# The set-up of mask and selector, and the order of four early steps, in a fused block-sparse attention and SoLU layer

## The chip, the cores and the metric

One NeuronCore of a Trainium2 chip runs the whole program. Its engines work side by side, each in the order of its own queue: TensorE (PE, with weight loads shown as PEld), VectorE (DVE), ScalarE (ACT), GpSimd (POOL), and SyncE (SP), which here only issues transfers. They wait for each other by semaphores. The metric is the device time of one execution in microseconds, lower is better.

## The reference, cut to what matters

Attention over 4 batches, 8 heads, 768 tokens and a head width of 64. The mask works on blocks of 32 tokens (24 x 24 blocks): neighbours, the first and last row and column of blocks, and three sampled blocks in each row of blocks are kept. The result goes, as 3072 tokens x 512, through a layer that is softmax-gated and normalised.

```
mask = np.abs(blk_i - blk_j) <= 1
mask |= (blk_i == 0) | (blk_j == 0) | (blk_i == n_blocks-1) | (blk_j == n_blocks-1)
for qb in range(n_blocks):
    for kb in sampled_blocks[qb]: mask[block qb, block kb] = True
scores = where(mask, q @ k.T / 8, -1e9);  attn = softmax(scores);  x = attn @ v
h = x @ w_in;  solu = h * softmax(h)
out = ((solu - mean) / sqrt(var + 1e-6) * g_ln) @ w_out
```

## The kernel before, in words

**Tiling.** A batch has four pairs of heads (`pr`) and three passes of 256 queries; a pass has 12 units, three for each pair. A unit `s` is 256 keys x 256 queries of both heads: four matmuls into the tile `sco` (L400), one exp of 128 x 1024 on ACT (L411) into `exs`, and eight matmuls against the values into `op` (L428). There are 144 units. `normalise` (L441, L442) divides by the row sums and writes `xb`. Behind each pass follows the layer for its two groups of 128 tokens: `x_turn` transposes `xb` by DMA into `xT`, `h` by eight matmuls (L470), `e` = exp(h) on ACT (L479), `solu` = h times e on DVE (L491), its transpose by DMA into `lnT` (L496), statistics (L505) and the root `rstd` (DVE L512 to L521, then POOL L523), `o` by eight matmuls (L530), scaling by `rstd` on DVE (L541), a store.

**The mask as rows of the operands.** K transposed and Q transposed (`KT`, `QT`) have 64 rows for the head and 24 more. In KT these hold a selector (1 where the token lies in the row's block), in QT the mask of that query against each block of keys (0 or -30000), so the score matmul adds the mask by itself. `stat_m` is the static part of the mask (24 x 24); six selections on POOL (L593) make it. `selT` (24 x 768) is the selector, made from ones by two selections (L596). Three DVE operations on 24 x 24 (`acc`, L613 and L616) mark the sampled blocks once `samp_i` has come from memory; L618 multiplies them into `mask_l`. Two matmuls (L632) spread `mask_l` over 768 queries into `m_ps`; two ACT copies (L662) write that into the mask rows of QT for the two heads of pair 0. DVE copies (`mask_rows`, L644) write the rows of the other pairs from there, and `selT` into KT.

**Pair 0** is loaded first: ACT casts K's first two chunks of 128 tokens, K's other four, then Q's first two (L320); `turn_mm` transposes by matmuls (L350), `turn_out` copies the result out of PSUM on DVE (L322). Pairs 1 to 3 are cast on POOL; `selector(pr)` (L650) writes the selector into the natural layout of K there, so that the turn brings it along. `zeros` issues matmuls on zeros (L605) whose result nobody reads.

**The order.** Up to the first scores the order in the text is the order on each engine. From there a planner sorts steps by a due time in units of `s` (`at(when, ...)`); the sorted order is each engine's queue, and nothing is reordered later. Queues are in order: a step that waits holds back all that stands behind it on its engine. `p_h` and `p_o` are PSUM tiles with one buffer each: a turn, an `h` or an `o` that takes one waits until the tile before has been read. `sco` has two buffers. The transfers of SP, loads and transposes alike, stand in one queue too. For batch 1 the lists `first` give due times for loads, casts, DMA turns (`pd_k`, `pd_q`) and `shift` copies on POOL (L322) of each pair.

**The first group's statistics** (`stats`, `rstd` of group 0 of pass 0, the `head` case) are due at es + 4.1, es being the due time of its exp, 20.5. The second group's `solu` is due at 27.0.

Of the kernel before, what the change touches and what calls it, by code (L numbers as in the profile page):

```python
# [7 lines left out]
FP32 = mybir.dt.float32  # L8
# [200 lines left out]
def kernel(  # L209
# [14 lines left out]
    BLK = 32  # L224
# [332 lines left out]
    with tc.manual_schedule():  # L557
# [18 lines left out]
        nc.vector.memset(selT, 1.0)  # L576
# [8 lines left out]
        nc.gpsimd.tensor_copy(out=io_f, in_=io_i)  # L585
        nc.gpsimd.affine_select(out=ident, in_=ident, compare_op=ALU.not_equal, fill=1.0,
                                base=0, channel_multiplier=1, pattern=[[-1, 128]])
        for fill, base, cm, step in (
            (NEG, 1, -1, 1), (NEG, 1, 1, -1),
            (0.0, -1, 1, 0), (0.0, NB - 2, -1, 0),  # L590
            (0.0, -1, 0, 1), (0.0, NB - 2, 0, -1),
        ):
            nc.gpsimd.affine_select(out=stat_m, in_=stat_m, compare_op=ALU.is_ge, fill=fill,  # L593
                                    base=base, channel_multiplier=cm, pattern=[[step, NB]])
        for base, sg in ((0, 1), (BLK - 1, -1)):
            nc.gpsimd.affine_select(out=selT, in_=selT, compare_op=ALU.is_ge, fill=0.0,  # L596
                                    base=base, channel_multiplier=-BLK * sg,
                                    pattern=[[sg, NCH], [NCH * sg, TQ]])

        def zeros(n, pool=p_o):  # L600
            w = pool
            if pool in (p_o, p_op):
                w = pool.tile([128, 512], FP32, tag="o" if pool is p_o else "op", name="warm")
            for _ in range(n):
                nc.tensor.matmul(w, zer[:, 0:128], zer, start=True, stop=True,  # L605
                                 skip_group_check=True)

        zeros(8)
# [6 lines left out]
        for r in range(1, NR):  # L615
            nc.vector.scalar_tensor_tensor(out=acc[r], in0=io_f, scalar=samp_f[:, r : r + 1],  # L616
                                           in1=acc[r - 1], op0=ALU.is_equal, op1=ALU.max)
        nc.vector.scalar_tensor_tensor(out=mask_l[:, D:KR], in0=acc[-1], scalar=0.0, in1=stat_m,  # L618
# [6 lines left out]
        cast(nc.scalar, 0, 0, "k", 0, 2, 0)  # L625
        cast(nc.scalar, 0, 0, "k", 2, NCH, 0)
        cast(nc.scalar, 0, 0, "q", 0, 2, 0)
# [3 lines left out]
        for i in range(2):  # L631
            nc.tensor.matmul(m_ps[0:KR, i, 0 : S // 2], mask_l,  # L632
                             sel_f[:, i * (S // 2) : (i + 1) * (S // 2)], start=True, stop=True)

        def rows(t, h0, h1):
            return t[D:KR].rearrange("p (h c) t -> p h (c t)", c=NCH)[:, h0:h1]

        def spread(x, n):
            return x.rearrange("p (o c) -> p o c", o=1).broadcast_to([NB, n, S])
# [16 lines left out]
        warm_t = p_sco.tile([128, 2, 512], FP32, tag="sco", name="warm_t")[:, 0, :]  # L656
        zeros(1, warm_t)
        turn_mm(0, 0, "k", p_op, 2, NCH)
        zeros(1, warm_t)
        turn_out(0, 0, "k", DVE2, 0, 2)  # L660
        for hh in range(2):
            nc.scalar.copy(  # L662
                out=rows(QT[0], hh, hh + 1).rearrange("p o (i c) -> p (o i) c", i=2),
                in_=m_ps[D:KR, :, 0 : S // 2])
        turn_mm(0, 0, "q", p_o, 0, 2)
        zeros(3, warm_t)
# [13 lines left out]
        def turn(when, b, pr, key, pool, c0=0, c1=NCH, engs=DVE2, later=0.02):  # L680
            at(when, turn_mm, b, pr, key, pool, c0, c1)
            at(when + later, turn_out, b, pr, key, engs, c0, c1)
# [10 lines left out]
        for pr, w0 in ((2, 2.85), (3, 5.85)):  # L693
            selector(pr)
            cast(nc.gpsimd, 0, pr, "k")
            cast(nc.gpsimd, 0, pr, "q", 0, 2)
            turn(w0, 0, pr, "k", p_h)
            turn(w0 + 0.05, 0, pr, "q", p_o, 0, 2)
# [3 lines left out]
        for pr, when in enumerate((8.9, 10.9, 12.4, 15.4)):  # L702
            turn(when, 0, pr, "q", p_o, 2, NCH, later=0.06)
        at(4.5, nc.gpsimd.memset, mean_w, 1.0 / d_ff)
        at(4.5, nc.gpsimd.memset, ones_c, 1.0)
        at(4.5, nc.gpsimd.memset, mhalf, -0.5)
# [44 lines left out]
        for s in range(n_units):  # L751
# [15 lines left out]
            [9.1, 9.2, 9.3, 9.4, 9.5, 9.6, 24.1, 24.11], [9.5, 9.6, 14.0, 14.1, 14.2, 14.3, 26.8, 27.6],  # L767
            [12.5, 12.6, 24.05, 24.06, 27.1, 27.2, 33.2, 36.1],
            [17.0, 17.1, 26.0, 27.2, 29.2, 30.1, 36.6, 39.0],
            [9.7, 24.12, 27.3, 27.4], [18.0, 28.5, 32.0, 33.0])  # L770
# [16 lines left out]
        def layer(ps, i, hs, es, os):  # L787
            for when, n0, n1 in hs:
                at(when, h_mms, ps, i, n0, n1)
            at(es, e_exp, ps, i)  # L790
            head = ps == 0 and i == 0
            at(es + (0.33 if head else 0.5), solu, ps, i)
            at(es + 0.55, ln_turn, ps, i)
            at(es + (4.1 if head else 1.7), stats, ps, i)
            at(es + (4.2 if head else 3.5), rstd, ps, i)
            for when, n0, n1 in os:
                at(when, o_mms, ps, i, n0, n1)
            at(os[-1][0] + 0.1, scaled, ps, i, nc.vector)
            at(os[-1][0] + 0.12, store, ps, i)
# [193 lines left out]
```

## Time and profile before

| what | value |
|---|---|
| three timed runs | 215.08, 215.62, 215.66 us; median 215.62 |
| profiled execution, its own time | 213.43 us |
| its span, first to last instruction | 211.8 us |
| granted TensorE clock, mean | 0.995 |
| DVE, POOL busy | 66%, 52% of the span |
| bytes read and written in HBM | 23.07 MB, 6.29 MB |
| first score matmul | 8.19 us |

A line of a timeline reads: start in us, length in us, engine, line of the kernel, operation, tile written <- tiles read, shape, how many were merged, and in brackets how long the engine had been idle before it and whose event ended that.

### The profile page before, as it was taken

The numbers are of one execution on the slowest core, as the hardware profiler recorded it, in microseconds if no ns is written. First come the engines' busy times: TensorE is split into PE (matmuls) and PEld (weight loads), VectorE is DVE, ScalarE is ACT, GpSimd is POOL, SyncE is SP. The second block draws the span as 40 slices with busy tenths as digits, with TensorE's granted clock in tenths as the row PEclk, the third lists the DMA queues.
The fourth block names the chain that finished last, engine by engine and source line by source line (L and its number), as shares of the span: only waits on it lengthen the run. The fifth ranks groups of instructions, "written<-read, shape, count | busy, mean of one in ns | idle before, by whom it ended". The sixth has DMA issues, their size and how long they took to land. (4 is left out here: it accounts for less than half of the span.)

```text
span 211.8 us, 5674 instructions
## 1 busy us (share of the span) xinstructions
PE 200.9 (95%) x2245; PEld 138.4 (65%) x2245; DVE 139.5 (66%) x328; ACT 175.7 (83%) x207; POOL 110.0 (52%) x157
## 2 busy tenths in 40 slices
PE   7898999978999999999999999999999999999991
PEld 2567877755766766766766676676676676765451
DVE  6875796985665574585575566667458457558782
ACT  6687989877798898898898899889889889877470
POOL 7999887768964385764465484575160110011111
PEclk9999999999999999999999999999999999999998
DMA  5999999789999789999989989989843275436404
GB/s 180 361 346 267 302 383 243 148 248 196 279 147 328 177 158 340 190 127 331 186 145 328 200 148 316 192 171 327 170 105 99 53 101 101 70 82 121 118 15 143
DMA packets 74291, 42.03 MB, mean 198 GB/s; under 512 B 56212, under 2 KB 69780, under 8 KB 74260
## 3 DMA queue, kind: packets, MB, share of 16 engines
q1 hardware_dynamic: 73316, 40.06, 79.4%
q0 software_dynamic: 528, 1.05, 2.6%
q10 hardware_dynamic: 416, 0.52, 0.8%
q8 instruction: 18, 0.29, 0.6%
q14 instruction: 13, 0.11, 0.2%
HBM read 23.07 MB, written 6.29 MB: 139 GB/s over the span
## 5 line engine op out<-in xcount | busy, mean ns | idle before, releaser
L411 ACT ACTIVATE exs<-sco 128x1024 bf16<-128x1024 f32 x144 | 141.6, 1024 | 10.4 <-PE sco L400 6.7
L400 PE MATMUL sco<-QT,KT 88*128 88x256 bf16 x576 | 86.6, 272 | 0.5 <-DVE QT L322 0.3
L400 PEld LDWEIGHTS <-KT 88*128 88x128 bf16 x576 | 55.0, 97 | 33.2 <-issue 5.1
L470 PE MATMUL h<-w_in_sb,xT 128*128 128x512 bf16 x176 | 55.2, 378 | 1.3 <-DVE solu L491 1.1
L428 PE MATMUL op<-VA,exs 128*128 128x65 bf16 x1152 | 52.0, 194 | 0.9 <-DVE KT L322 0.7
L428 PEld LDWEIGHTS <-exs 128*128 128x128 bf16 x1152 | 48.8, 97 | 4.3 <-PE sco L400 0.9
L530 PE MATMUL o<-w_cen_sb,lnT 128*128 128x512 bf16 x176 | 45.2, 379 | 0.9 <-DMA lnT<-solu 0.9
L523 POOL TENSOR_TENSOR rstd<-vpe,mhalf 128x1 f32<-128x1 f32 x24 | 13.2, 548 | 50.7 <-DVE vpe L521 44.9
L441 DVE RECIPROCAL recip_all<-op 128x4 f32<-128x4 f32 x48 | 8.7, 181 | 43.9 <-PE op L428 43.8
L479 ACT ACTIVATE e<-h 128x1024 bf16<-128x1024 f32 x22 | 22.5, 1023 | 13.4 <-PE h L470 11.9
L505 DVE BATCH_NORM_STATS2 stats<-solu 128x6 f32<-128x512 bf16 x48 | 30.7, 681 | 0.0
L322 POOL COPY KT<-pd_k 64x768 bf16<-64x768 bf16 x24 | 19.7, 821 | 19.0 <-DMA pd_k<-kn 16.6
L491 DVE TENSOR_TENSOR solu<-h,e 128x1024 bf16<-128x1024 f32 x22 | 26.8, 1216 | 3.4 <-ACT e L479 3.4
L530 PEld LDWEIGHTS <-lnT 128*128 128x128 bf16 x176 | 15.8, 98 | 14.5 <-DMA lnT<-solu 1.2
L322 POOL COPY QT<-pd_q 64x768 bf16<-64x768 bf16 x24 | 20.5, 855 | 5.7 <-DMA pd_q<-qn 4.7
L541 DVE TENSOR_SCALAR ot<-o,rstd 128x512 f32<-128x512 f32 x20 | 15.0, 750 | 12.1 <-issue 6.3
L442 DVE TENSOR_TENSOR xb<-op,recip_all 128x256 bf16<-128x256 f32 x48 | 20.4, 424 | 1.7
L470 PEld LDWEIGHTS <-xT 128*128 128x128 bf16 x176 | 15.6, 98 | 5.6 <-issue 1.4
L322 POOL CAST qn<-st_q 128x768 bf16<-128x768 f32 (+2 forms) x19 | 14.0, 746 | 6.4 <-DMA st_q<-in_q_dram 5.8
L322 POOL CAST kn<-st_k 128x768 bf16<-128x768 f32 x15 | 13.1, 870 | 7.6 <-DMA st_k<-in_k_dram 7.3
L322 POOL CAST VA<-st_v 128x768 bf16<-128x768 f32 x16 | 13.4, 848 | 4.8 <-DMA st_v<-in_v_dram 4.6
L605 PE MATMUL warm<-zer 128*128 128x512 bf16 x16 | 6.0, 505 | 1.4 <-DVE zer L571 1.4
(85 smaller groups left out, 114.5 us busy)
## 6 DMA issues: line engine op xcount, KB each, us to landing
st_v<-in_v_dram SPq DMA_DIRECT2D x16, 384.0 KB, 5.7
out_dram<-ot SPq DMA_DIRECT2D x23, 256.0 KB, 3.8
st_k<-in_k_dram SPq DMA_DIRECT2D x15, 384.0 KB, 5.0
st_q<-in_q_dram SPq DMA_DIRECT2D x12, 384.0 KB, 4.9
w_out_f<-in_moe_w_out_dram SPq DMA_DIRECT2D x4, 512.0 KB, 11.3
st_q<-in_q_dram SPq DMA_DIRECT2D x4, 256.0 KB, 6.9
w_in_sb<-in_moe_w_in_dram POOLq DMA_DIRECT2D x1, 1024.0 KB, 12.8
st_q<-in_q_dram SPq DMA_DIRECT2D x4, 128.0 KB, 4.1
```

The lines of the kernel that those rows point to most:

```text
L322: eng.tensor_copy(out=o, in_=i)
L400: nc.tensor.matmul(sco[:, hh, kk * QW : (kk + 1) * QW], KT[b % 2][0:KR, h * NCH + 2 * u + kk, :], QT[b % 2][0:KR, h * NCH + PC * j : h * N ...
L411: nc.scalar.activation(out=exs_of[ps, pr][:, u].rearrange("p a b c -> p (a b c)"), in_=sco_of.pop(s).rearrange("p a b -> p (a b)"), func=A ...
L428: nc.tensor.matmul(op[:, hh, ic, :], exs[:, u, hh, kk, ic * TQ : (ic + 1) * TQ], VA[b % 2][:, 2 * pr + hh, 2 * u + kk, :], start=(u == 0 a ...
L442: nc.vector.tensor_tensor(out=xb_of[ps][:, :, 2 * pr * D : 2 * (pr + 1) * D].rearrange("p c (h d) -> p h c d", h=2), in0=op[:, :, :, 0:D], ...
L470: nc.tensor.matmul(h_of[ps, i][:, half, :], xT_of[ps][:, i * KD + c, :], w_in_sb[:, c, half * HF : (half + 1) * HF], start=(c == 0), stop= ...
L479: nc.scalar.activation(out=o, in_=h, func=ACT.Exp, scale=1.0, accum_out=esum_all[:, t : t + 1])
L491: nc.vector.tensor_mul(out=so, in0=h, in1=e)
L505: nc.vector.bn_stats(out=stat_of[ps, i][:, half, :], in_=so[:, half, :])
L523: nc.gpsimd.tensor_tensor(out=rstd_of[ps, i], in0=vpe, in1=mhalf, op=ALU.pow)
L530: nc.tensor.matmul(ops_of[ps, i], lnT_of[ps, i][:, c, :], w_cen_sb[:, c, :], start=(c == 0), stop=(c == KF - 1), skip_group_check=True)
L541: nc.vector.tensor_scalar(out=o, in0=i_, scalar1=r, scalar2=None, op0=ALU.mult)
```

## The change

Five things are edited; what is computed stays the same.

- The selector `selT` is made first on POOL, from the zero tile `zer` (no fill of ones on DVE); then `stat_m` by three selections, with two small DVE fills (24 x 2 and 1 x 24) just ahead of `mask_l` for the rows that the other three selections made; then `ident`. Three fills of constants (`mean_w`, `ones_c`, `mhalf`) move from unit 4.5 to here.
- ACT casts Q's first chunks ahead of K's last four. The mask product is split at 256 columns (256 and 512 in place of 384 twice); three ACT copies (the first 256 columns for both heads, then 512 for each head) take the place of two of 768. Q's turn stands ahead of K's second turn on PE, and three matmuls on zeros fewer are issued in all.
- Pair 3's turns are due at 5.81 and 5.82 in place of 5.85 and 5.90: ahead of the last value matmuls of pair 0 and its `normalise`. The second half of pair 2's Q turn is due at 12.9 in place of 12.4: behind the scores of unit 14.
- The first statistics are due at es + 6.6 and 6.7: on DVE they stand behind the second group's `solu`.
- Batch 1: loads of K and Q of pair 3 and of V of pair 1 are due at 27.06 to 27.08 in place of 24.1 to 24.12, on SP behind the second group's `lnT`. Casts of pair 3 are due at 27.6 and 27.7 (26.8 and 27.6 before), shifts of Q of pair 1 at 27.3 (27.2) and of K of pair 2 at 30.05 (29.2). On POOL the first `rstd` now stands behind the copies of `pd_k` of pair 1, and the second `rstd` behind the cast of V of pair 1 and ahead of the copies of `pd_k` of pair 2.

```diff
@@ -573,7 +573,6 @@
         stat_m = fix.tile([NB, NB], FP32, name="stat_m")
         nc.vector.memset(stat_m, 0.0)
         selT = fix.tile([NB, NCH, TQ], BF16, name="selT")
-        nc.vector.memset(selT, 1.0)
         mask_l = fix.tile([NB, KR], BF16, name="mask_l")
         nc.vector.memset(mask_l, 0.0)
         for t in VA:
@@ -583,19 +582,20 @@
         nc.gpsimd.iota(io_i, pattern=[[1, NB]], base=0, channel_multiplier=0)
         io_f = fix.tile([NB, NB], FP32, name="io_f")
         nc.gpsimd.tensor_copy(out=io_f, in_=io_i)
+        zer_b = zer[0:NB, 0:TQ].rearrange("p (o t) -> p o t", o=1).broadcast_to([NB, NCH, TQ])
+        for src, fill, base, sg in ((zer_b, 1.0, -1, -1), (selT, 0.0, BLK - 1, -1)):
+            cm = BLK
+            nc.gpsimd.affine_select(out=selT, in_=src, compare_op=ALU.is_ge, fill=fill,
+                                    base=base, channel_multiplier=cm,
+                                    pattern=[[sg, NCH], [NCH * sg, TQ]])
+        for fill, base, cm, step in ((NEG, 1, -1, 1), (NEG, 1, 1, -1), (0.0, NB - 2, -1, 0)):
+            nc.gpsimd.affine_select(out=stat_m, in_=stat_m, compare_op=ALU.is_ge, fill=fill,
+                                    base=base, channel_multiplier=cm, pattern=[[step, NB]])
         nc.gpsimd.affine_select(out=ident, in_=ident, compare_op=ALU.not_equal, fill=1.0,
                                 base=0, channel_multiplier=1, pattern=[[-1, 128]])
-        for fill, base, cm, step in (
-            (NEG, 1, -1, 1), (NEG, 1, 1, -1),
-            (0.0, -1, 1, 0), (0.0, NB - 2, -1, 0),
-            (0.0, -1, 0, 1), (0.0, NB - 2, 0, -1),
-        ):
-            nc.gpsimd.affine_select(out=stat_m, in_=stat_m, compare_op=ALU.is_ge, fill=fill,
-                                    base=base, channel_multiplier=cm, pattern=[[step, NB]])
-        for base, sg in ((0, 1), (BLK - 1, -1)):
-            nc.gpsimd.affine_select(out=selT, in_=selT, compare_op=ALU.is_ge, fill=0.0,
-                                    base=base, channel_multiplier=-BLK * sg,
-                                    pattern=[[sg, NCH], [NCH * sg, TQ]])
+        nc.gpsimd.memset(mean_w, 1.0 / d_ff)
+        nc.gpsimd.memset(ones_c, 1.0)
+        nc.gpsimd.memset(mhalf, -0.5)
 
         def zeros(n, pool=p_o):
             w = pool
@@ -605,7 +605,7 @@
                 nc.tensor.matmul(w, zer[:, 0:128], zer, start=True, stop=True,
                                  skip_group_check=True)
 
-        zeros(8)
+        zeros(7)
 
         samp_f = fix.tile([NB, NR], FP32, name="samp_f")
         nc.vector.tensor_copy(out=samp_f, in_=samp_i[:, :, 0])
@@ -615,6 +615,8 @@
         for r in range(1, NR):
             nc.vector.scalar_tensor_tensor(out=acc[r], in0=io_f, scalar=samp_f[:, r : r + 1],
                                            in1=acc[r - 1], op0=ALU.is_equal, op1=ALU.max)
+        nc.vector.memset(stat_m[:, 0 : NB : NB - 1], 0.0)
+        nc.vector.memset(stat_m[0:1, :], 0.0)
         nc.vector.scalar_tensor_tensor(out=mask_l[:, D:KR], in0=acc[-1], scalar=0.0, in1=stat_m,
                                        op0=ALU.is_equal, op1=ALU.mult)
         for pr in range(1, NP):
@@ -623,20 +625,21 @@
                 in_=zer[:, 0 : NCH * 2 * NB].rearrange("p (x r) -> p x r", r=NB),
                 func=ACT.Copy, scale=0.0, bias=1.0)
         cast(nc.scalar, 0, 0, "k", 0, 2, 0)
+        cast(nc.scalar, 0, 0, "q", 0, 2, 0)
         cast(nc.scalar, 0, 0, "k", 2, NCH, 0)
-        cast(nc.scalar, 0, 0, "q", 0, 2, 0)
+        warm_t = p_sco.tile([128, 2, 512], FP32, tag="sco", name="warm_t")[:, 0, :]
         turn_mm(0, 0, "k", p_h, 0, 2)
         m_ps = p_sco.tile([TQ, 2, 512], FP32, tag="sco", name="m_ps")
         sel_f = selT.rearrange("p c t -> p (c t)")
-        for i in range(2):
-            nc.tensor.matmul(m_ps[0:KR, i, 0 : S // 2], mask_l,
-                             sel_f[:, i * (S // 2) : (i + 1) * (S // 2)], start=True, stop=True)
+        for i, x0, x1 in ((0, 0, QW), (1, QW, S)):
+            nc.tensor.matmul(m_ps[0:KR, i, 0 : x1 - x0], mask_l, sel_f[:, x0:x1],
+                             start=True, stop=True)
 
         def rows(t, h0, h1):
             return t[D:KR].rearrange("p (h c) t -> p h (c t)", c=NCH)[:, h0:h1]
 
         def spread(x, n):
-            return x.rearrange("p (o c) -> p o c", o=1).broadcast_to([NB, n, S])
+            return x.rearrange("p (o c) -> p o c", o=1).broadcast_to([NB, n, x.shape[-1]])
 
         row_q = QT[0][D:KR, 0:NCH, :].rearrange("p c t -> p (c t)")
 
@@ -653,17 +656,14 @@
 
         selector(1)
         mask_rows(nc.vector, KT[0], 0)
-        warm_t = p_sco.tile([128, 2, 512], FP32, tag="sco", name="warm_t")[:, 0, :]
+        turn_mm(0, 0, "q", p_o, 0, 2)
         zeros(1, warm_t)
         turn_mm(0, 0, "k", p_op, 2, NCH)
-        zeros(1, warm_t)
+        zeros(2, warm_t)
         turn_out(0, 0, "k", DVE2, 0, 2)
-        for hh in range(2):
-            nc.scalar.copy(
-                out=rows(QT[0], hh, hh + 1).rearrange("p o (i c) -> p (o i) c", i=2),
-                in_=m_ps[D:KR, :, 0 : S // 2])
-        turn_mm(0, 0, "q", p_o, 0, 2)
-        zeros(3, warm_t)
+        for h0, n, i, x0, x1 in ((0, 2, 0, 0, QW), (0, 1, 1, QW, S), (1, 1, 1, QW, S)):
+            nc.scalar.copy(out=rows(QT[0], h0, h0 + n)[:, :, x0:x1],
+                           in_=spread(m_ps[D:KR, i, 0 : x1 - x0], n))
         turn_out(0, 0, "q", DVE2, 0, 2)
         turn_out(0, 0, "k", DVE2, 2, NCH)
         mask_rows(nc.vector, QT[0], 2)
@@ -690,20 +690,17 @@
 
         for pr in (2, 3):
             at(1.01, mask_rows, nc.vector, QT[0], 2 * pr)
-        for pr, w0 in ((2, 2.85), (3, 5.85)):
+        for pr, w0, dw in ((2, 2.85, 0.05), (3, 5.81, 0.01)):
             selector(pr)
             cast(nc.gpsimd, 0, pr, "k")
             cast(nc.gpsimd, 0, pr, "q", 0, 2)
             turn(w0, 0, pr, "k", p_h)
-            turn(w0 + 0.05, 0, pr, "q", p_o, 0, 2)
+            turn(w0 + dw, 0, pr, "q", p_o, 0, 2)
         for pr in range(NP):
             at(2.0 + 0.1 * pr, cast, nc.gpsimd, 0, pr, "v")
             at(5.0 + 0.1 * pr, cast, nc.gpsimd, 0, pr, "q", 2, NCH)
-        for pr, when in enumerate((8.9, 10.9, 12.4, 15.4)):
+        for pr, when in enumerate((8.9, 10.9, 12.9, 15.4)):
             turn(when, 0, pr, "q", p_o, 2, NCH, later=0.06)
-        at(4.5, nc.gpsimd.memset, mean_w, 1.0 / d_ff)
-        at(4.5, nc.gpsimd.memset, ones_c, 1.0)
-        at(4.5, nc.gpsimd.memset, mhalf, -0.5)
         for n in range(4):
             at(n + 0.9, zeros, 2, p_op)
 
@@ -764,10 +761,10 @@
         kq = [(key, pr) for pr in range(NP) for key in "kq"]
         vs = [("v", pr) for pr in range(NP)]
         first = (
-            [9.1, 9.2, 9.3, 9.4, 9.5, 9.6, 24.1, 24.11], [9.5, 9.6, 14.0, 14.1, 14.2, 14.3, 26.8, 27.6],
+            [9.1, 9.2, 9.3, 9.4, 9.5, 9.6, 27.06, 27.07], [9.5, 9.6, 14.0, 14.1, 14.2, 14.3, 27.6, 27.7],
             [12.5, 12.6, 24.05, 24.06, 27.1, 27.2, 33.2, 36.1],
-            [17.0, 17.1, 26.0, 27.2, 29.2, 30.1, 36.6, 39.0],
-            [9.7, 24.12, 27.3, 27.4], [18.0, 28.5, 32.0, 33.0])
+            [17.0, 17.1, 26.0, 27.3, 30.05, 30.1, 36.6, 39.0],
+            [9.7, 27.08, 27.3, 27.4], [18.0, 28.5, 32.0, 33.0])
         then = (
             [3.2, 4.1, 5.0, 5.9, 15.2, 16.1, 17.9, 27.2], [8.2, 9.4, 10.6, 11.8, 20.2, 21.4, 23.8, 32.2],
             [9.3, 13.0, 14.0, 20.9, 25.0, 26.0, 37.0, 38.0],
@@ -791,8 +788,8 @@
             head = ps == 0 and i == 0
             at(es + (0.33 if head else 0.5), solu, ps, i)
             at(es + 0.55, ln_turn, ps, i)
-            at(es + (4.1 if head else 1.7), stats, ps, i)
-            at(es + (4.2 if head else 3.5), rstd, ps, i)
+            at(es + (6.6 if head else 1.7), stats, ps, i)
+            at(es + (6.7 if head else 3.5), rstd, ps, i)
             for when, n0, n1 in os:
                 at(when, o_mms, ps, i, n0, n1)
             at(os[-1][0] + 0.1, scaled, ps, i, nc.vector)
```

## The prediction

> **What bounds the kernel now.** I first read ACT's own timeline, because every unit needs one exp of 1.02 us there and its idle time shows where units are late.
>
> ```profile
> 8.82 5.05 ACT L411 ACTIVATE exs<-sco 128x1024 bf16<-128x1024 f32 x5 [0.69 <-PE sco L400]
> 25.01 6.04 ACT L411 ACTIVATE exs<-sco 128x1024 bf16<-128x1024 f32 x6 [0.40 <-PE sco L400]
> 45.51 3.25 ACT L411 ACTIVATE exs<-sco 128x1024 bf16<-128x1024 f32 x3 [1.31 <-PE sco L400]
> 73.75 1.02 ACT L479 ACTIVATE e<-h 128x1024 bf16<-128x1024 f32 x1 [0.57 <-PE h L470]
> 81.43 1.02 ACT L479 ACTIVATE e<-h 128x1024 bf16<-128x1024 f32 x1 [0.57 <-PE h L470]
> ```
>
> From 66 to 181 us the pattern repeats every 7.68 us (81.43 less 73.75), and each wait there is for PE; the page gives PE 95% of the span. What the change can save lies ahead of 66 us: the first exp comes at 8.82, and the early layer exps (32.67, 40.35, 49.33, 57.99, 66.08) are 7.68, 8.98, 8.66 and 8.09 apart, 33.41 us in all, 2.7 more than four regular periods. A gain that is still there at 66 us reaches the end whole, as nothing of the change lies behind it.
>
> Next, the timeline of the first 9 us.
>
> ```profile
> 3.17 0.91 DVE L613 TENSOR_SCALAR acc<-io_f,samp_f 24x24 f32<-24x24 f32 x1
> 3.20 0.85 POOL L596 TENSOR_SCALAR_AFFINE_SELECT selT<-selT 24x768 bf16<-24x768 bf16 x1
> ...
> 4.12 0.89 DVE L616 SCALAR_TENSOR_TENSOR acc<-io_f,samp_f,acc 24x24 f32<-24x24 f32 x1
> 4.12 0.85 POOL L596 TENSOR_SCALAR_AFFINE_SELECT selT<-selT 24x768 bf16<-24x768 bf16 x1
> ...
> 4.94 1.09 POOL L650 TENSOR_SCALAR_AFFINE_SELECT kn<-kn 128x288 bf16<-128x288 bf16 x2
> ...
> 5.56 0.48 DVE L618 SCALAR_TENSOR_TENSOR mask_l<-acc,stat_m 24x24 bf16<-24x24 f32 x1
> 6.65 1.48 ACT L662 CAST QT<-m_ps 24x768 bf16<-24x768 f32 x2 [1.16 <-PE m_ps L632]
> ```
>
> The DVE operations on 24 elements take as long as the POOL selection beside them: 3.17 to 4.08 beside 3.20 to 4.05, then 4.12 to 5.01 beside 4.12 to 4.97; `mask_l` ends at 6.04, the second selection of `kn` at 6.03. At the end of the kernel, with POOL idle, such an operation (L895) takes 0.18 in the chain of waits. So the mask is late because long selections of POOL run beside it. Behind it come `m_ps` (6.09), the ACT copies, the scores at 8.19 and the exp at 8.82.
>
> Last, the timeline from 40 to 62 us, and the rows of the load of `w_in`.
>
> ```profile
> 40.84 1.28 DVE L505 BATCH_NORM_STATS2 stats<-solu 128x6 f32<-128x512 bf16 x2
> 43.02 1.22 DVE L491 TENSOR_TENSOR solu<-h,e 128x1024 bf16<-128x1024 f32 x1
> 44.26 1.36 SPq L496 DMA_TRANSPOSE lnT<-solu  x1
> 44.38 0.59 PE L470 MATMUL h<-w_in_sb,xT 128*128 128x512 bf16 x2 [1.08 <-DVE solu L491]
> 50.77 1.69 PE L530 MATMUL o<-w_cen_sb,lnT 128*128 128x512 bf16 x7 [0.79 <-DMA lnT<-solu]
> 57.03 1.24 SPq L453 DMA_TRANSPOSE xT<-xb  x1
> 61.12 0.60 PE L470 MATMUL h<-w_in_sb,xT 128*128 128x512 bf16 x2 [0.23 <-DMA xT<-xb]
> ```
> ```profile
> L711 POOL DMA_DIRECT2D w_in_sb<-in_moe_w_in_dram x1: 969/969/969, 13.7 to 13.7; - x1
> DMA to landing us min/median/max: 12.8/12.8/12.8
> ```
>
> PE waits 1.08 us because the second `solu` stands behind the first statistics, 0.79 for a transpose that stands behind three loads in SP's queue, 0.23 for `xT`. `w_in` lands at 13.7 + 12.8 = 26.5; the first `h` begins at 27.80.
>
> **The change part by part.** *Mask.* POOL now makes `selT` from 1.46 to 3.23 (two at a pitch of 0.92), `stat_m` to 4.0 (three at 0.26), `ident` to 4.3, the three fills (0.27, from 16.99 to 17.26 before) to 4.6. At 3.17, when `acc` begins (fixed by the landing of `samp_i`), the long selections are over, so I let each DVE operation end with a short one of POOL: `acc` at 3.5, 3.75, 4.0. The two fills on DVE are not in the trace; the nearest row, the fill of 24 x 24, takes 0.08, so 0.2 with the hand-over. `mask_l` ends near 4.5 in place of 6.04. If DVE stays as slow as now, it ends at 6.2.
>
> *To the first exp.* With the mask early, others end last. K's first cast waits for its load until 4.26 and ends at 4.67; Q's (0.40) at 5.1 (its load, 1.42 + 3.2, is there at 4.65); K's rest at 5.6. PE's slow early pitch, 0.43 for 512 columns (eight in 3.60), gives `m_ps` from 4.97 to 5.6, Q's turn to 5.85, read from 6.05; DVE copies it in 0.61 and is done at 6.7. On PE the zeros and K's second turn end near 6.8, if the faster pitch of 0.22 holds from 6.1, as now. Scores at 6.8; exp 0.63 behind, as from 8.19 to 8.82: 7.45. ACT's three copies (0.52 each, scaled from 1.48 for 1536 columns, so 5.5 to 7.15) hide under this. Gain 1.4. Ends: 0.3 (PE slow throughout: 0.21 more on one zero matmul, 0.2 on the turn, 0.43 on two, 0.2 on the first scores), 1.7 (ACT's copies alone).
>
> POOL gains only 0.2 to 0.5 behind this: the load of K of pair 1 lands at 1.89 + 4.2 = 6.1, just when its cast begins now (6.12). The turns of pairs 1 to 3 stay covered, their casts ending a microsecond or more ahead.
>
> *Pair 3's turns* go past eight matmuls (0.41), so the copies on DVE, now behind `normalise` (16.68 to 17.31), start 0.25 sooner, and the scores that wait for them too: 0.25. `normalise` moves behind them, 1.4 us later; its tile is next needed at 20.15. *The half turn of pair 2* waits 0.35 on PE for DVE's copy of the one before, and ACT then 0.40; behind unit 14's scores that wait is covered: 0.4. Sum up to 26 us: 2.05.
>
> *The wall at w_in.* The first `h` would then begin at 25.75. The load is issued by POOL perhaps 0.4 sooner, so it lands near 26.1: 0.4 is given back, 1.65 left. The bounds are 0 (as fast as compute) and 0.75 (issued no sooner).
>
> *The first statistics.* With them behind it, the second `solu` starts when `xb` is done, 41.7 in place of 43.02 (times of before, all shifted alike), and PE's 1.08 goes. Late next: the statistics and their small operations (40.84 to 42.55, so 1.7) end at 44.6, POOL's `rstd` behind two copies of 0.82 near 45.2, the scaling (0.75), the next statistics and `normalise` at 47.9; PE wants that tile at 48.30 - 1.08 = 47.2 and stands 0.7. `lnT` now goes ahead of the loads, so the 0.79 goes too: 1.2 to the good near 50.
>
> *The wall at xT.* SP has no rest from 38.56 to 56.03, and the transfers are serial: what is issued is the same, and `lnT` costs SP a wait of 0.45 for `solu`. It reaches `xT` at 56.5 in place of 57.03, as `xb` is ready before that. So `xT` lands at about 60.6 in place of 61.1, and of the 1.2 there stay 0.45. Bounds: -0.4 (landing later by the wait) and 2.0 (no wall: the 2.7 us of lateness less the 0.7).
>
> Removed and hidden: the fill of ones (0.70 on DVE, ahead of the wait for `samp_i`), three selections of `stat_m` (0.78 on POOL). The moved loads cost nothing while K of pair 3 is cast by 49.4 for a transpose at 53.50.
>
> Sum: 1.4 + 0.25 + 0.4 - 0.4 + 0.45 = 2.1. The profiled execution is 213.43 (span 211.8 and 1.6 around it), so 211.3. The timed runs lie higher, median 215.62; the 2.1 taken from there gives **213.5**. Bounds put together: front 0.95 to 2.35, second part -0.4 to 2.0, so 211.3 to 215.1.
>
> The slow early pitch is in the rows: 0.43 up to 4.3 us, 0.22 from 6.8. The Trainium skill, TensorE: Matmul & The Clock Gate, Part 1 ("The HAM clock gate"), says that the array runs at half clock until a window of about 3.4 us was busy, that the window runs freely, and that the point of change so varies from run to run. The trace agrees with the two pitches. By the rule the change may come as late as 1.37 + 6.8 = 8.2 us, an estimate from that page; then the 1.4 would be 0.3 and the sum 1.0 + 0.45, so 214.2.
>
> **The rivals.** *No walls:* `w_in` lands in time and transfers have room (their share was 0.34 to 0.85 of the time between 38 and 46 us). 2.05 + 1.2 = 3.25: 212.4. Against it: before, PE already waited for `xT`. *The start hardly moves:* PE stays slow, or DVE goes on waiting for POOL. 0.3 + 0.25 + 0.4 + 0.45 = 1.4: 214.2. For it: POOL is still busy without a gap. *All is given back:* the transfers of the first 62 us, 0.9 or more busy in all but 8 us, end when they did; `xT` still lands at 61.1 on the clock and PE with it: 215.6. Against it: SP idled for 2.1 us ahead of the transpose at 38.56, waiting for compute. *Slower:* the second `rstd` now stands on POOL behind the cast of V of pair 1, which waits for a load moved behind `lnT`. DVE's scaling waits for that `rstd`, and `xb`, `xT` and `h` for DVE: from landing to `xT` 0.82 + 0.6 + 0.75 + 0.55 + 1.29 + 0.7 = 4.7 us. I expect it at 50.6; from 52.3 it sets `xT`, from 53.9 it eats the front's gain too. Issued at 45.7 with the longest landing of such a load (9.0) it comes at 54.7, `xT` 2.4 us late: 215.62 - 1.65 + 2.4 = 216.4. Against it: the same load landed in 6.2 before.
>
> **How the numbers follow.** Forecast 0.48, no walls 0.16, small start 0.14, given back 0.13, slower 0.09. Less than 0.3% (0.65 us) can't be told from no change. Faster: the first three but a rest of 0.01, 0.77; same: 0.14; slower: 0.09. The range runs from 212.1, past the no-walls time, to 215.4, so that it leaves out the slower case and about half of the one that gives all back.
>
> **What would show it.** Right: `mask_l` ends below 5 us; first exp at 7.2 to 7.8; the first `h` waits for `w_in`; no wait for `solu` near 43 nor for `lnT` near 50; a wait for `xb` of about 0.7, and one for `xT` of 0.3 or more. Wrong: `acc` still as long as POOL's operations; PE's pitch 0.43 beyond 7 us; the scaling late by V's load; new waits behind 66 us.

## The result, and the profile after

Over 20 runs of each kernel on one chip the changed kernel took 213.8 us (median, all but one within 212.0 to 215.0) and the kernel before 215.19: a ratio of 0.9932, 95% interval 0.9905 to 0.9958. The forecast was 213.5. Ratios and intervals, here and below, leave out runs more than 1.5% above the fastest of their kernel, so they are not exactly those of the medians. The two profiled executions stand the other way round: 214.49 us for the changed kernel (span 212.9) against 213.43 for the one before (span 211.8). One execution is one draw, and those of a kernel lie some 3 us apart: before's was below the fastest of its 20 timed runs (213.55), after's 0.7 above its median. So the profiles are read for mechanisms, several executions of each kernel side by side, and the timed runs for sums.

ACT's timeline of the changed kernel (start, length, engine, line, tiles; in brackets the idle time ahead and what ended it):

```profile
8.77 1.02 ACT L411 ACTIVATE exs<-sco 128x1024 bf16<-128x1024 f32 x1 [1.34 <-PE sco L400]
...
14.94 2.99 ACT L411 ACTIVATE exs<-sco 128x1024 bf16<-128x1024 f32 x3 [0.50 <-PE sco L400]
...
40.67 1.02 ACT L479 ACTIVATE e<-h 128x1024 bf16<-128x1024 f32 x1 [0.57 <-PE h L470]
...
72.69 1.02 ACT L479 ACTIVATE e<-h 128x1024 bf16<-128x1024 f32 x1 [0.57 <-PE h L470]
```

The first exp is no sooner than before (8.77 and 8.82), the exp of unit 5 even later (14.94 and 14.46). The gain comes in the middle: from the second layer exp (40.67) to the sixth (72.69) it is 32.02 us, before 33.40.

The same kernel's timeline of the first 8 us, DVE, POOL and PE:

```profile
1.37 3.17 PE L605 MATMUL warm<-zer 128*128 128x512 bf16 x7 [1.37 <-DVE zer L571]
2.31 0.85 POOL L588 TENSOR_SCALAR_AFFINE_SELECT selT<-selT 24x768 bf16<-24x768 bf16 x1
2.51 0.68 DVE L611 CAST samp_f<-samp_i 24x3 f32<-24x3 int32 x1 [0.62 <-DMA samp_i<-in_sampled_blocks_dram]
3.30 0.23 DVE L613 TENSOR_SCALAR acc<-io_f,samp_f 24x24 f32<-24x24 f32 x1
4.35 0.47 DVE L620 SCALAR_TENSOR_TENSOR mask_l<-acc,stat_m 24x24 bf16<-24x24 f32 x1
4.98 0.86 PE L635 MATMUL m_ps<-selT,mask_l 24*88 24x256 bf16 x2
5.97 0.63 PE L605 MATMUL warm_t<-zer 128*128 128x512 bf16 x1
6.93 0.82 POOL L322 CAST kn<-st_k 128x768 bf16<-128x768 f32 x1 [1.15 <-DMA st_k<-in_k_dram]
```

`acc` takes 0.23 now that only short selections run beside it (0.91 before), and `mask_l` ends at 4.82. The long selection of `selT` now meets the cast of `samp_i`, which takes 0.68 (0.16 before). On PE a zero matmul still takes 0.63 at 5.97; before, such a one took 0.39 at 6.54. PE's slow pitch lasted to 10.24 us here. And POOL, done with its selections at 5.78, waits 1.15 us for the load of K of pair 1.

And its timeline from 41 to 62 us, DVE, PE and SP's queue:

```profile
41.93 1.22 DVE L491 TENSOR_TENSOR solu<-h,e 128x1024 bf16<-128x1024 f32 x1
43.17 1.23 SPq L496 DMA_TRANSPOSE lnT<-solu  x1
43.46 0.59 PE L470 MATMUL h<-w_in_sb,xT 128*128 128x512 bf16 x2
...
48.07 0.68 PE L428 MATMUL op<-VA,exs 128*128 128x65 bf16 x16 [0.42 <-DVE xb L442]
49.49 1.67 PE L530 MATMUL o<-w_cen_sb,lnT 128*128 128x512 bf16 x7
52.18 0.75 DVE L541 TENSOR_SCALAR ot<-o,rstd 128x512 f32<-128x512 f32 x1 [0.72 <-POOL rstd L523]
...
55.38 1.34 SPq L453 DMA_TRANSPOSE xT<-xb  x1
60.06 0.60 PE L470 MATMUL h<-w_in_sb,xT 128*128 128x512 bf16 x2 [0.50 <-DMA xT<-xb]
```

PE's waits for `solu` (1.08) and `lnT` (0.79) are gone, a wait for `xb` of 0.42 has come and the one for `xT` has grown from 0.23 to 0.50, as forecast; `xT` is issued 1.65 us sooner than before.

### The profile page after: what moved, and what is told of

Read it like the earlier page. It is cut to its first block, busy times and chain, and to the rows that moved or that the text cites. A ratio compares the mean times of both kernels' runs of the same rounds, so it can differ in the third digit from the quotient of the medians.

```text
span 212.9 us, 5667 instructions
## 1 busy us (share of the span) xinstructions
PE 202.9 (95%) x2242; PEld 139.3 (65%) x2242; DVE 137.9 (65%) x329; ACT 176.0 (83%) x208; POOL 108.6 (51%) x154
## 5 line engine op out<-in xcount | busy, mean ns | idle before, releaser
L400 PE MATMUL sco<-QT,KT 88*128 88x256 bf16 x576 | 87.5, 273 | 1.7 <-POOL QT L322 1.3
L523 POOL TENSOR_TENSOR rstd<-vpe,mhalf 128x1 f32<-128x1 f32 x24 | 13.1, 548 | 48.2 <-DVE vpe L521 42.9
L491 DVE TENSOR_TENSOR solu<-h,e 128x1024 bf16<-128x1024 f32 x22 | 26.8, 1216 | 3.7 <-ACT e L479 3.7
L322 POOL COPY QT<-pd_q 64x768 bf16<-64x768 bf16 x24 | 19.7, 821 | 5.0 <-DMA pd_q<-qn 3.9
L322 POOL CAST VA<-st_v 128x768 bf16<-128x768 f32 x16 | 13.4, 849 | 5.4 <-DMA st_v<-in_v_dram 5.2
L322 POOL CAST kn<-st_k 128x768 bf16<-128x768 f32 x15 | 12.4, 829 | 6.5 <-DMA st_k<-in_k_dram 6.2
L719 POOL TENSOR_SCALAR w_out_sb<-w_out_f,g_ln_sb 128x512 bf16<-128x512 f32 x8 | 6.2, 786 | 2.6 <-DMA w_out_f<-in_moe_w_out_dram 2.5
## 6 DMA issues: line engine op xcount, KB each, us to landing
w_in_sb<-in_moe_w_in_dram POOLq DMA_DIRECT2D x1, 1024.0 KB, 12.9
```

Source lines behind the costliest of these rows:

```text
L322: eng.tensor_copy(out=o, in_=i)
L400: nc.tensor.matmul(sco[:, hh, kk * QW : (kk + 1) * QW], KT[b % 2][0:KR, h * NCH + 2 * u + kk, :], QT[b % 2][0:KR, h * NCH + PC * j : h * N ...
L491: nc.vector.tensor_mul(out=so, in0=h, in1=e)
L523: nc.gpsimd.tensor_tensor(out=rstd_of[ps, i], in0=vpe, in1=mhalf, op=ALU.pow)
```

## The experiments

Twelve kernels ran, four at a time on one chip, beside runs of the kernel before (35, 35 and 29 of them). The table holds all; times within a run are us from its trace, units count from 0 (what the expectations call the fifth exp is that of unit 5). "Pitch" is when PE's matmuls changed from the slow pitch (0.43 for 512 columns) to the fast one (0.22). Each ratio is to the runs of before beside it, whose median was 214.16 for e1 to e4, 214.74 for e5 to e9 and 214.47 for e10 to e13. e5, the kernel before against itself, shows what an interval is worth: 1.0002, some 0.4% to either side. "2nd to 6th" is from the second layer exp to the sixth, "rest" from there to the end of the span.

| run | median us, ratio to before [95%] | pitch | exp of unit 0, of unit 5 | `w_in` lands, first `h` | 2nd layer exp | 2nd to 6th | rest |
|---|---|---|---|---|---|---|---|
| before | 215.19 | 5.04 | 8.82, 14.46 | 26.50, 27.80 | 40.35 | 33.40 | 138.1 |
| after | 213.80, 0.9932 [0.9905, 0.9958] | 10.24 | 8.77, 14.94 | 27.05, 28.13 | 40.67 | 32.02 | 140.2 |
| e1_after8 | 212.55, 0.9937 [0.9909, 0.9965] | 5.46 | 8.05, 13.44 | 27.40, 27.44 | 39.98 | 31.96 | 140.8 |
| e2_start_only | 215.24, 1.0077 [1.0046, 1.0108] | 4.10 | 7.65, 13.44 | 27.18, 27.22 | 39.77 | 33.53 | 139.6 |
| e3_second_only | 214.58, 1.0025 [0.9993, 1.0056] | 6.74 | 8.36, 14.16 | 27.67, 27.71 | 40.26 | 32.72 | 140.0 |
| e4_after_again | 214.11, 1.0009 [0.9976, 1.0043] | 9.92 | 8.72, 14.76 | 27.42, 27.76 | 40.31 | 32.57 | 140.0 |
| e5_before_again | 214.14, 1.0002 [0.9958, 1.0046] | 5.94 | 8.18, 13.56 | 27.20, 27.24 | 39.78 | 32.90 | 139.2 |
| e6_start8 | 215.33, 1.0026 [0.9988, 1.0063] | 4.22 | 7.76, 13.60 | 27.26, 27.30 | 39.84 | 33.13 | 139.6 |
| e8_before_filled | 214.16, 1.0003 [0.9962, 1.0044] | 6.68 | 9.03, 14.41 | 27.82, 27.86 | 40.41 | 33.44 | 139.2 |
| e9_win_early | 213.01, 0.9946 [0.9907, 0.9985] | 7.17 | 8.23, 13.62 | 24.93, 27.06 | 39.61 | 32.03 | 139.4 |
| e10_after_third | 213.86, 0.9973 [0.9934, 1.0012] | 4.17 | 7.74, 13.13 | 27.18, 27.22 | 39.76 | 32.90 | 139.6 |
| e11_after8_again | 213.19, 0.9938 [0.9897, 0.9979] | 5.90 | 8.23, 13.62 | 26.77, 26.81 | 39.35 | 32.59 | 139.5 |
| e12_stats_only8 | 219.66, 1.0247 [1.0172, 1.0322] | 4.46 | 7.71, 13.59 | 27.64, 27.68 | 40.22 | 37.34 | 140.2 |
| e13_lists_only8 | 215.42, 1.0067 [1.0031, 1.0103] | 4.47 | 7.71, 13.44 | 27.59, 27.63 | 40.17 | 34.23 | 139.7 |

### PE's pitch and the eighth zero

e1 is the changed kernel with one zero matmul more ahead of the first turn; e4 is the changed kernel again.

```diff
-        zeros(7)
+        zeros(8)
```

> The changed kernel with eight zero matmuls in place of seven at the start. Theory (clock step): in the profiled execution of the changed kernel matmuls of 512 columns kept a pitch of 0.43 us until 10.2 us (5.0 in the one of before), and that ate the 1.4 us of the start; PE had stood still from 4.33 to 4.66, which the eighth closes, so PE is busy without a gap from 1.37 to 8 us and the pitch halves by 8.2 us at the latest: first exp at 7.4 to 8.2, second at 8.5 to 9.3, time 0.5 to 1.5 us under the changed kernel, so a ratio to before of 0.986 to 0.991. Rival (loads): the load of K of pair 1 landed at 6.9 in place of 6.1 and holds the second exp; then an eighth zero does nothing and the ratio stays 0.993 or above.

> The changed kernel once more. Theory (clock step, its place by chance): ratio 0.993 plus or minus 0.003, and in this execution the pitch of 0.43 us ends at another time than 10.2 us, somewhere from 7 to 13; where it ends before 9 us the layer exp of 33.0 comes sooner by 0.5 or more. Rival (place set by the kernel): it ends at 10.2 again. The single late load that cost 1.6 us at 111 us in the profile of the changed kernel is not expected at the same place; if it is there again, it belongs to the change.

e4's pitch changed at 9.92, nearly as late as in the first profile (10.24); e1's at 5.46, and its exp of unit 5 came 1.3 to 1.5 us sooner than in the two. PE's timeline of e1:

```profile
1.37 3.60 PE L605 MATMUL warm<-zer 128*128 128x512 bf16 x8 [1.37 <-DVE zer L571]
5.84 0.38 PE L605 MATMUL warm_t<-zer 128*128 128x512 bf16 x1
7.42 0.60 PE L400 MATMUL sco<-QT,KT 88*128 88x256 bf16 x4 [0.54 <-ACT QT L665]
```

With seven zeros the last starts at 3.90 and, at the pitch of 0.43, ends at 4.33 (ends of matmuls in the view are modelled and lie later); PE's first turn, which waits for ACT's cast, begins at 4.66 (4.63 in e10). The eighth fills that gap. In e1 the zero at 5.84 already takes 0.38, where after's at 5.97 took 0.63, and what the first scores wait for is ACT's mask copy. e1's first exp (8.05) came as its theory had it, its ratio did not: 0.9937, where 0.986 to 0.991 was expected and the rival had 0.993 or above. On this chip e1's interval lies below e4's. Both were run again, on another chip:

> The changed kernel once more, as it is. Two executions of it so far kept PE's slow pitch (0.427 us for 512 columns) until 10.24 and 9.92 us, and its medians stood at 0.9932 and 1.0009 of the kernel before. Theory A, the seven zeros leave too little in a window, so the pitch changes late whenever the windows lie badly: in this profile either again near 10 us, with the fifth exp near 14.8, or, where the windows lie well, by 7 us with the fifth exp near 13.5; median 0.995 to 1.001 of before, and 0.3 to 0.8 us above the kernel with eight zeros in the same call. Rival B, the difference between the two kernels' medians was chance: within 0.3 us of each other here, at 0.993 of before both.

> The changed kernel with one zero matmul more ahead of the first turn, so that PE stands no 0.3 us at 4.3. Theory A: pitch changes by 7 us, fifth exp 13.4 to 13.6, exp of the second layer group (e of the first pass, second group) near 39.9, median about 0.994 of before, as the first time (0.9937). Rival B: as the changed kernel to 0.3 us.

This time the changed kernel's pitch changed at 4.17 and its exp of unit 5 came at 13.13, the soonest of all. So seven zeros do not always cost: it depends on the execution. The medians stand 0.7 us apart again (213.86 and 213.19), though these intervals overlap.

e2 and e6 are one more such pair: the kernel before with the edits of the start alone (mask, casts, split, order on PE), with seven and with eight zeros. Against the changed kernel, with the two lists and the two lines of the statistics as before too:

```diff
-        for pr, w0, dw in ((2, 2.85, 0.05), (3, 5.81, 0.01)):
+        for pr, w0 in ((2, 2.85), (3, 5.85)):
...
-        for pr, when in enumerate((8.9, 10.9, 12.9, 15.4)):
+        for pr, when in enumerate((8.9, 10.9, 12.4, 15.4)):
```

e8 is the kernel before with two zeros more behind the first turn, meant to fill the 0.92 us that PE stood idle ahead of `m_ps` in the first profile.

```diff
         turn_mm(0, 0, "k", p_h, 0, 2)
+        zeros(2)
```

> The kernel before with the edits of the start alone (mask, selector, order of the casts, split product, seven zeros); turns of pairs 2 and 3, statistics and the list for batch 1 as before. Theory (clock step): mask_l ends below 5 us in each execution, but with PE's slow pitch lasting to 8 us or beyond the first exp comes between 7.4 and 8.8 and the next ones no sooner than before: ratio 0.995 to 1.001. Rival (the prediction's sum): the start's 1.4 us arrives less the 0.4 of the wall at w_in: ratio 0.993 to 0.996. Either way DMA landings of w_in at 26 to 27 us.

> The start edits alone (turns, statistics and list of batch 1 as before), but with eight zero matmuls. Theory (clock step): with seven the ratio was 1.008; the eighth takes back some 1 to 1.5 us, so 0.997 to 1.002, with the pitch of PE halved by 8.2 us and the first exp at 7.4 to 8.1. Theory of the wall: the first h begins when w_in lands, at 27.1 to 27.7, whatever the first exp. Rival: the eighth zero is worth nothing and the 0.7% between the changed kernel with seven and with eight was noise: 1.005 or above.

> The kernel before with two zero matmuls more behind the first turn, in the 1.0 us in which PE stands still before the mask product. Theory (clock step): the slow pitch ends by 7.2 us in each execution; before, it may last to 10 us in some, so a ratio of 0.994 to 0.999. Rival (the start does not matter, as w_in lands late anyway): 0.999 to 1.002, with the first h at the landing of w_in.

The ratios with eight zeros are lower than those with seven in all three pairs, by 0.0072, 0.0035 and 0.0051 (the last pair, e2 and e6, did not run side by side). But the first 0.9932 of the changed kernel, with seven, is as low as any with eight. The differences are about 1 us, near what the late pitch cost at unit 5. It can't be seen in a timed run when its pitch changed, so that this is the cause of the pairs' difference is likely and not shown; e2's own trace has the change at 4.10 and nothing that explains why it is 0.8% slower than before, outside both of its expectations. e8 brought nothing, and did not test what it was made for: in its execution `mask_l` ended at 5.02, so there was no idle time to fill, and the two zeros only held the mask product until 5.96 (5.11 in e5, the kernel before without them). Its first exp is the latest of all.

### The start alone, and the wall at `w_in`

e6's first exp is at 7.76, a microsecond sooner than in the first profile of before, and yet it was no faster (1.0026). Three things bear on that.

First, the kernel before was run again:

> The kernel before, unchanged, against itself: a ratio of 1.000 is expected, and how far it lies from it says what a ratio of this kind is good for. Its profile is a second execution of the kernel before. Theory (chance): the 1.6 to 2 us that the executions profiled since lose near 105 to 112 us, where scores wait for a copy of a transposed Q of batch 2, come here too, and the first profile of before was a lucky one without them. Rival: they belong to the edits, and here each step between layer exps from 66 to 180 us is 7.68 again.

Its timeline, DVE and POOL:

```profile
2.84 0.23 DVE L613 TENSOR_SCALAR acc<-io_f,samp_f 24x24 f32<-24x24 f32 x1
3.10 0.99 DVE L616 SCALAR_TENSOR_TENSOR acc<-io_f,samp_f,acc 24x24 f32<-24x24 f32 x2
3.20 1.78 POOL L596 TENSOR_SCALAR_AFFINE_SELECT selT<-selT 24x768 bf16<-24x768 bf16 x2
4.20 0.81 DVE L618 SCALAR_TENSOR_TENSOR mask_l<-acc,stat_m 24x24 bf16<-24x24 f32 x1
```

`samp_i` landed sooner than in the first profile, so `acc` began at 2.84 in place of 3.17 and slipped in ahead of POOL's long selections; only the operations behind it still met them, and `mask_l` ended at 5.01. It did so in e3 (5.01) and e8 (5.02) too, which have before's start. The 6.04 of the first profile was the exception; with the new start it was 4.81 or 4.82 in all ten traces. The mask edit is worth 0.2 us mostly, and 1.2 now and then.

Second, the load of K of pair 1. With the new start POOL waited for it in all ten traces, 0.45 to 1.32 us, and the cast began at 6.23 to 7.10; with the old start it began at 6.12 to 6.96. So POOL, which issues the load of `w_in` behind its casts, was no sooner there. In e2, e6 and e12, with first exps of 7.65 to 7.76, PE's turn of pair 1 waited 0.20 to 0.29 for that cast, and the second exp came 1.5 to 1.6 us behind the first.

Third, the load of `w_in` itself. PE's timeline of e10:

```profile
27.22 0.38 PE L470 MATMUL h<-w_in_sb,xT 128*128 128x512 bf16 x1 [0.65 <-DMA w_in_sb<-in_moe_w_in_dram]
```

In ten of the fourteen traces the first `h` starts 0.04 us behind the landing of `w_in`, at 26.8 to 27.9, whatever the first exp did; in six of them, all with the new start, PE visibly waited for it (0.20 to 1.10). The load was issued at 13.4 to 14.2 and landed 12.8 to 14.2 later, with either start (e9 apart). e9 is e1 with that load issued ahead of the cast of V on POOL:

```diff
-        at(2.05, w_load_in)
+        at(1.99, w_load_in)
```

> The changed kernel with eight zeros, and the load of w_in issued by POOL ahead of the first cast of V in place of behind it. Theory (wall at w_in): with eight zeros PE waited 0.9 us for w_in, which landed at 27.4; issued 1.1 us sooner it lands near 26.3, the wait is 0 to 0.2 and the layer exp at 32.3 comes 0.6 to 0.9 sooner; ratio 0.988 to 0.992 (0.9937 without). Rival (the transfers share one bandwidth): w_in lands sooner by 0.3 at most, or the loads beside it come later by as much, and the ratio stays 0.992 to 0.995.

Issued at 13.1 it landed at 24.93, and PE no longer waited for it:

```profile
27.06 0.38 PE L470 MATMUL h<-w_in_sb,xT 128*128 128x512 bf16 x1
```

The first `h` came 0.4 sooner than in e1, the second layer exp likewise (39.61 and 39.98), and its span of 211.1 us is the shortest of all. So the wait was real, but only 0.4 of its 0.91 us came back; the ratio, 0.9946, missed the 0.988 to 0.992 of the theory and lies in the rival's range, though the load landed 2.5 us sooner and not 0.3. It can't be told from e1's (0.9937), which had other runs beside it: that the wall costs time at the end of the kernel is not shown.

### The second part, whole and in halves

e3 is the kernel before with the first statistics' due times and batch 1's lists alone; against before:

```diff
-            [9.1, 9.2, 9.3, 9.4, 9.5, 9.6, 24.1, 24.11], [9.5, 9.6, 14.0, 14.1, 14.2, 14.3, 26.8, 27.6],
+            [9.1, 9.2, 9.3, 9.4, 9.5, 9.6, 27.06, 27.07], [9.5, 9.6, 14.0, 14.1, 14.2, 14.3, 27.6, 27.7],
...
-            [17.0, 17.1, 26.0, 27.2, 29.2, 30.1, 36.6, 39.0],
-            [9.7, 24.12, 27.3, 27.4], [18.0, 28.5, 32.0, 33.0])
+            [17.0, 17.1, 26.0, 27.3, 30.05, 30.1, 36.6, 39.0],
+            [9.7, 27.08, 27.3, 27.4], [18.0, 28.5, 32.0, 33.0])
...
-            at(es + (4.1 if head else 1.7), stats, ps, i)
-            at(es + (4.2 if head else 3.5), rstd, ps, i)
+            at(es + (6.6 if head else 1.7), stats, ps, i)
+            at(es + (6.7 if head else 3.5), rstd, ps, i)
```

> The kernel before with the first statistics behind the second solu and the new list for batch 1 alone; start and turns as before. Theory: the second part is worth more than the 0.45 us predicted, as the profile of the changed kernel shows 1.4 us from the layer exp at 40.7 to the one at 72.7 (32.0 us in place of 33.4): ratio 0.993 to 0.995, with the waits for solu and for lnT near 43 and 50 us gone and a wait for xT near 60 of about 0.5. Rival (wall at xT as predicted): 0.45 us, ratio 0.998.

From the second layer exp to the sixth it took 32.72. The five traces without this part took 33.28 in the mean (32.90 to 33.53), the seven that have all of it 32.40 (31.96 to 32.90): it saves 0.9 in this stretch. e3's time (1.0025) shows none of it: both of its expectations, 0.993 to 0.995 and 0.998, were missed. Then the halves, in the changed kernel with eight zeros: in e12 the first four lines with a plus (the lists) are put back, in e13 the last two (the statistics).

> The changed kernel with eight zeros, but batch 1's lists of due times as before: of the second part only the first statistics' move is left, so the three loads stand ahead of the second lnT in SP's queue again. From the second layer exp to the sixth the kernels without the second part took 33.28 us (mean of five), those with the whole of it 32.26 (mean of five). Theory A, the wait for solu is the part that counts and the wait for lnT is covered by the wall at xT: about 32.3, PE's wait for lnT of 0.5 to 0.8 back, time as the whole. Theory B, the lists carry the gain, as they let xT land sooner: about 33.0, time 0.7 above the kernel with both. Theory C, each alone is given back at xT or xb, and only both together bring it: about 33.2 here and in the next run.

> The changed kernel with eight zeros, but the first statistics ahead of the second solu, as before: of the second part only batch 1's lists are left. From the second layer exp to the sixth: theory A (statistics carry it) about 33.0, with PE's wait for solu of 1.1 back and none for lnT; theory B (lists carry it) about 32.4; theory C (only both together) about 33.2. Time accordingly: A 0.7 us above the kernel with both, B as that.

Each half makes the kernel slower than before, by 2.5% and 0.7%; beside the kernel with both (e11, 0.9938 on the same chip) it is 3.1% and 1.3%. The stretch took 37.34 and 34.23 us, more than any of the three theories had: a half is not only less of the gain, it puts steps in a bad order. The timeline of e12, POOL, DVE and PE:

```profile
46.25 0.82 POOL L322 CAST kn<-st_k 128x768 bf16<-128x768 f32 x1 [2.06 <-DMA st_k<-in_k_dram]
47.02 1.70 POOL L322 COPY QT<-pd_q 64x768 bf16<-64x768 bf16 x2
48.81 0.57 POOL L523 TENSOR_TENSOR rstd<-vpe,mhalf 128x1 f32<-128x1 f32 x1
49.41 0.75 DVE L541 TENSOR_SCALAR ot<-o,rstd 128x512 f32<-128x512 f32 x1 [5.10 <-POOL rstd L523]
51.95 0.86 PE L428 MATMUL op<-VA,exs 128*128 128x65 bf16 x16 [4.75 <-DVE xb L442]
```

With the old lists the cast of K of pair 3 is due at 26.8, ahead of the moved `rstd` (27.2). It waits 2.06 us for its load, `rstd` stands behind it on POOL, the scaling waits 5.10 for `rstd` on DVE, `normalise` stands behind the scaling, and PE waits 4.75 for the tile. The idle time seems to cost a second time: behind it the granted clock is 0.50, from 52.25 to 55.66 us, and four score matmuls take 1.06 at 53.04, 0.60 at 56.51. No other trace has such a stretch in its middle. All six timed runs of e12 have a mean granted clock of 0.977 to 0.989 (before: 0.994 or more), so its 2.5% is likely order and clock together. The new due times of the casts (27.6, 27.7) are there to let `rstd` pass. The timeline of e13, same engines:

```profile
44.20 0.59 PE L470 MATMUL h<-w_in_sb,xT 128*128 128x512 bf16 x2 [1.08 <-DVE solu L491]
49.99 0.82 POOL L322 CAST kn<-st_k 128x768 bf16<-128x768 f32 x1 [3.55 <-DMA st_k<-in_k_dram]
...
53.12 0.55 POOL L523 TENSOR_TENSOR rstd<-vpe,mhalf 128x1 f32<-128x1 f32 x1
53.71 0.75 DVE L541 TENSOR_SCALAR ot<-o,rstd 128x512 f32<-128x512 f32 x1 [2.11 <-POOL rstd L523]
```

Here `solu` is late as before, so `lnT` and the loads behind it go out late; K's cast waits 3.55, V's cast behind it 0.48, the second `rstd` stands behind both and ends at 53.7, and the scaling waits 2.11. This is the mechanism of the prediction's slower rival, from a late `solu` rather than a long load.

### What lies behind 66 us

In the changed kernel's trace PE has new waits there, for the copy of Q of the next batch:

```profile
110.86 0.38 PE L400 MATMUL sco<-QT,KT 88*128 88x256 bf16 x2 [0.79 <-POOL QT L322]
111.74 0.38 PE L400 MATMUL sco<-QT,KT 88*128 88x256 bf16 x2 [0.50 <-POOL QT L322]
```

Before's first trace has no such wait: its even steps of 7.68 us were peculiar to that execution. In twelve of the fourteen traces the step between layer exps that begins at 102 to 108 us takes 8.8 to 9.3, among them e2, e6 and e8, which lack the second part; e5, the kernel before again, has a step of 8.8 at another place, from 134 to 143. So the second part is not what brings this long step. The rest behind the sixth layer exp is 139.1 us in the mean of the five traces without the second part (138.1 to 139.6) and 139.9 in the seven with all of it (139.4 to 140.8). So up to 0.8 us of what is won by 73 us may be given back here; whether the second part causes that difference, or these few executions fell so, stays open. It would fit that neither the start alone (e6) nor the second part alone (e3) showed a gain in the timed runs, whose intervals are some 0.35% to either side.

## Why the prediction was right, and where its terms were not

The time (213.8 against 213.5) and the sign came out on the first chip. Run twice more, the same code stood at 1.0009 and 0.9973, both intervals with 1 inside them and well short of the 2.1 us of the sum. The changed kernel's median was nearly the same all three times (213.80, 214.11, 213.86); the kernel before's was not (215.19, 214.16, 214.47). Whether the chip or chance made that, the runs do not show; the number was hit with some luck. Step by step:

- *Mask.* The mechanism held: `acc` fell from 0.91 to 0.23 and `mask_l` came at 4.82 (forecast 4.5). Its baseline did not: the 6.04 was peculiar to that execution, and 5.01 is what before mostly does.
- *To the first exp, 1.4.* Mis-sized, the largest miss: the first exp came at 8.06 in the mean of ten traces with the new start, at 8.60 in four with the old, so 0.5, and the forecast 7.45 was never reached (best 7.65). Part of the 1.4 was the late mask of one execution. In the profiled execution the rival of the slow pitch came true: first exp at 8.77. The prediction's working took PE's faster pitch from 6.1 on "as now" and passed over the fact that the edit drops a zero just where PE then stands idle.
- *POOL behind the start, 0.2 to 0.5.* It gained nothing. The step had K of pair 1 land at 6.1, from one profile; its cast waited for it until 6.23 to 7.10, and the turns of pair 1 were not always covered.
- *Pair 3's turns, 0.25.* Right: from the exp of unit 5 to that of unit 9 took 5.26 to 5.30 without the edit and 5.00 with it in six of eight traces.
- *The half turn, 0.4.* ACT's idle time fell from 0.40 to 0.24 only; in the first trace of the changed kernel PE then waited 0.35 for the copy of `xT` (L463).
- *The wall at `w_in`, -0.4.* The mechanism was right, the landing was not. The step expected the load 0.4 us sooner, landing at 26.1. It landed at 26.8 to 27.6 with the new start (e9 apart), no sooner than the 26.5 to 27.8 with the old, as POOL was no sooner there. The second layer exp came at 40.2 in the mean of four traces with the old start, at 40.0 in ten with the new: of 1.65 us that should have been left, 0.2 was. This is the rival in which the start hardly moves, though by this wall in most executions and by the slow pitch in two.
- *First statistics and the wall at `xT`, 0.45.* The steps came as worked out: no wait for `solu` or `lnT`, one for `xb` of 0.42 (0.7 foreseen), V's load there at 45.60 + 5.2 = 50.8 (50.6 foreseen, with 52.3 as the point from which it sets `xT`), the second `rstd` right behind its cast at 51.59, `xT` waited for 0.50. But `xT` landed at 60.0, not 60.6, and the part was worth 0.9 up to the sixth layer exp.
- *A gain at 66 us reaches the end whole.* Not shown: what lies behind has waits of its own in every trace but one, and that one was the profile that the prediction read.

So the start brought 0.2 in place of 1.65 and the second part 0.9 in place of 0.45, 1.1 together in place of 2.1, with up to 0.8 perhaps given back. The misses are of opposite sign but do not cancel. That the time still fitted owes something to the base as well: the 2.1 was taken from 215.62, the median of three runs, where twenty gave 215.19. The clock rule from the Trainium skill (TensorE: Matmul & The Clock Gate, Part 1, "The HAM clock gate") was weighed as a rival and would have been the better guide to the first profile: the estimate from it was a change as late as 8.2 us; it came at 10.24. That section gives about half a microsecond either way for how the moment varies; here it ranged from 4.10 to 10.24 over fourteen executions of a few kernels, so the measurement decides.

## What to carry to other kernels

Before a gain at the start is added up, look for the next fixed arrival on its way (here a 1 MB load needed at 27 us) and look at whether that can be moved too; here moving it took the wait away, though a gain in time at the end is not shown. Two steps that stand in several queues are moved together or not at all: either half of this move lost 0.7 to 2.5%, the whole won 0.9 us in its stretch. And before a gain in the middle is counted in full, see whether what lies behind keeps it. Where a term rests on the landing time of one transfer (here `samp_i`, K of pair 1, `w_in`), take a second profile of the kernel before and only then believe it.

## What was not expected of the hardware

PE's change of pitch looks decided by how full stretches of about 3.4 us are. Counted back from the change in steps of 3.41 us (the length that the same section of the Trainium skill gives), the stretch that closes at the change was 73% to 100% full of matmuls on 88 or 128 rows, and those that closed without a change 70% or less (64% in the changed kernel's first profile, with its gap at 4.33 and the 24-row `m_ps`). The traces agree with the length: in their records of the granted clock the fast spell lasts 59 to 61 times 3.413 us up to the change at the kernel's end, and in e12 it breaks off after 14 such stretches for exactly one at 0.50. Counting `m_ps` as busy would put the stretches of the changed kernel's two slow traces at 83% and 85%, above e2's 80% that sufficed, so that a matmul on 24 rows seems to count for little. This is read from fourteen traces and was not tried by itself. The profile's own clock row gives 1.00 for the first 5 us of the changed kernel: the record of the granted clock begins only at the change, in all fourteen traces, so ahead of it the slow pitch shows only in the spacing of the matmuls.
